# Squares and products of a two-layer transformer kernel placed on VectorE or GpSimd by the kernel's planner

## The chip, the cores and the metric

The kernel runs on one core of a Trainium2 chip. The time is that of one execution on the device in microseconds (us); the kernel before took 835.92 us, the median of three runs (835.25 to 836.88). The engines are called as in the profile: PE is TensorE (matmuls), PEld its weight loads, DVE is VectorE, ACT is ScalarE, POOL is GpSimd, SP is the engine whose queue issues the DMAs.

## The reference

Two layers, each of attention and a squared-ReLU network, over x of [1, 2048, 448] in bf16, with 16 heads of 28 columns and 1792 hidden units; both layers share their weights.

```python
def _A_ref(x, wqkv, wo):
    qkv = (x @ wqkv).reshape(B, S, 3, H, Dh).transpose(2, 0, 3, 1, 4)
    q, k, v = qkv[0], qkv[1], qkv[2]
    scores = jnp.einsum("bhqd,bhkd->bhqk", q, k) * Dh ** -0.5
    p = _softmax(scores, axis=-1)
    o = jnp.einsum("bhqk,bhkd->bhqd", p, v)
    return o.transpose(0, 2, 1, 3).reshape(B, S, D) @ wo

def _B_ref(x, w1, b1, w2, b2):
    h = jnp.einsum("bsd,df->bsf", x, w1) + b1
    r = jnp.where(h > 0, h, 0)
    return jnp.einsum("bsf,fd->bsd", r * r, w2) + b2

x = x + _A_ref(_layernorm(x), A_wqkv, A_wo)
x = x + _B_ref(_layernorm(x), B_w1, B_b1, B_w2, B_b2)
# and both lines once more
```

## The kernel before

**Work and tiles.** The 16 heads are four groups of four; a head has 32 rows of the array, so four heads share it. A *bank* is one PSUM bank of scores: 128 partitions by 512 fp32, which is one head with 256 queries and two blocks of 128 keys. PE makes the scores of three banks (`s_stream`, L956) into one of two tiles `sc`. The exponentials of a bank go one of two ways:

- On ACT: one activation (`e_stream`, L986) makes bf16 weights `pt` of all three banks of a tile, or of two banks when the third goes the other way.
- On VectorE's route: `a_unit` and `a_rest` make the exponential by bit arithmetic in four steps. The first step on DVE (L1034) shifts and clamps the scores into an fp32 tile in SBUF (`v_w`, or a piece of `K_sb`) and with that frees the PSUM bank. POOL (L1051) makes a linear function of the low 16 bits, in bf16 (`pd`, which lies in `pt`, `V_sb`, `h` or a tile of its own). DVE squares that in place (L1057, `bend`). DVE's closing step (L1064) adds the two and writes the bits of the bf16 result.

Then PE multiplies the weights with V (`p_stream`, L1127); 32 columns of V hold 28 of the head and ones, which give the sums of the softmax. For most blocks of 256 queries the result is copied to SBUF (L1154, L1156), the sums go through small DMAs on SP's queue and come back as inverse sums spread over partitions, and one product (`norm_pair`, L1255) for each pair of groups writes `oTn`. `chain` takes it from there: matmuls with wo, the addition to x (L1264), layer norm (L528, L533 on DVE; L555, L556 on POOL for the inverse root; L649 on DVE), W1 with ReLU (L1322) and square (L1331) on DVE, W2, again L1264, and for layer 1 the layer norm and the Q, K and V of layer 2. The work of `chain` runs beside the attention of later blocks, so that ACT has exponentials from start to end.

**What sets the order.** The program is written by a planner in Python (`Planner.run`). Each step is an `Op` with an engine, an estimated duration, what it depends on and what buffer it takes; streams of Ops have priorities. The planner always emits the Op that can start earliest by its own clocks. The engines then run their lists in this order. What matters here:

- `port=True` marks Ops of DVE and POOL that it does not let start while the other engine runs an Op so marked; it then moves the start to the end of that Op. L1051, L1057, L1064, L1255, L1331 and L649 are so marked.
- An Op may have several engines; `earliest` then takes the first, unless a later one could start earlier by more than a margin.
- `apart` decides whether a bank goes VectorE's route. One of its conditions is that DVE's queue in the plan is below an entry of the table `PACE`, which has 128 entries over the length of the program:

```python
if max(0.0, pl.clock["DVE"] - now) + left[0] > PACE[i * len(PACE) // len(units)]:
    return None
```

- `warm` adds up PE's load over the last 1.8 us (`TICK`); where it is low, `heat` (L1552) and `s_stream` emit matmuls whose result is not used, to keep PE's clock up. An Op's load is 0.9 (`SHARE`) of its duration unless its field `w` says otherwise.
- `sums` (L406) makes column sums of W1 once, between the layers, by 56 matmuls of one column; the last half block needs them.

Of the kernel before, what the change touches and what calls it, by code (L numbers as in the profile page):

```python
# [13 lines left out]
ALU = mybir.AluOpType  # L14
# [17 lines left out]
SHARE = 0.9  # L32
YL = 0.05
GN = 0.718
GM = 1.275
GS = 1.3
NORMG = 0
GM_ON = 0
GS_ON = 0
GS_STOP = 100  # L40
EXP_MID = 0.50773
EXP_LOW = 128.0 * 128
EXP_SHIFT = 184.0 * 128
# [39 lines left out]
LEAD = 15  # L83
LAST = 690
BUSY = 0.995
PACE = (2.2, 2.2, 2.2, 2.2, 1.8, 2.2, 2.2, 1.4, 3.0, 1.4, 1.4, 1.4, 2.2, 3.2, 3.6, 2.2, 2.2, 2.2, 2.2, 2.2, 0.6, 3.4, 2.6, 1.8, 1.0, 1.8, 2.6, 2.6, 2.2, 3.8, 3.0, 2.2, 2.2, 3.6, 2.2, 0.6, 3.0, 1.8, 1.8, 1.8, 1.8, 2.6, 2.2, 2.2, 1.4, 3.4, 2.6, 1.0, 2.2, 3.4, 3.6, 3.6, 1.4, 2.2, 3.0, 2.6, 3.8, 3.4, 1.8, 1.0, 2.6, 2.6, 2.2, 2.2, 3.8, 3.0, 1.8, 1.0, 3.8, 3.0, 1.8, 2.2, 2.2, 1.4, 3.2, 4.4, 2.6, 3.6, 3.6, 1.4, 1.8, 3.6, 3.0, 3.0, 3.0, 3.0, 2.2, 2.2, 2.2, 2.2, 3.0, 3.0, 1.8, 2.2, 2.6, 2.6, 1.4, 1.4, 4.0, 3.6, 3.6, 1.8, 1.8, 2.2, 2.2, 3.6, 1.4, 1.4, 2.2, 4.0, 1.8, 1.4, 2.2, 1.8, 2.6, 2.6, 2.2, 2.2, 2.6, 2.2, 2.8, 3.2, 1.4, 1.8, 1.8, 2.2, 2.2, 2.2)
SPAN = 11
NPT = 11
NOS = 2
# [39 lines left out]


class Op:
    __slots__ = ("eng", "dur", "fn", "deps", "acq", "rel", "mode", "sets", "start", "end", "res", "turn", "ready", "lat", "need", "got", "more", "room", "port", "base", "w")

    def __init__(self, eng, dur, fn, deps=(), acq=None, rel=None, mode="full", sets=(), lat=0.0, need=1, port=False):
        self.eng = eng if isinstance(eng, tuple) else (eng,)
        self.dur, self.fn, self.deps, self.mode, self.lat = dur, fn, deps, mode, lat
        self.rel = rel if isinstance(rel, list) else ([] if rel is None else [rel])
        self.acq = acq if isinstance(acq, tuple) or callable(acq) else (() if acq is None else (acq,))
        self.sets = sets if isinstance(sets, list) else ([sets] if sets else [])
        self.start = self.end = self.res = self.turn = None  # L140
        self.need, self.got, self.more, self.port, self.base = need, [], 0.0, port, None
        self.w = None
# [5 lines left out]
class Planner:  # L148
# [28 lines left out]
    def earliest(self, o):  # L177
        t = o.base
        if t is None:
            t = 0.0  # L180
            for d in o.deps:
                if not isinstance(d, Op):
                    d = self.tok.get(d)
                if d is None or d.end is None:
                    return None, None
                same = d.eng[0] == o.eng[0] and len(o.eng) == 1
                t = max(t, d.end + d.lat + ((0.03 if same else 0.10) if d.eng[0] == "DVE" else
                                    (0.0 if same and d.eng[0] != "DMA" else LAT[d.eng[0]])))
            o.base = t
        acq = o.acq() if callable(o.acq) else o.acq  # L190
        if o.acq:
            free = [r.when() for r in acq if r.when() is not None]
            if not free:
                return None, None
            t = max(t, min(free))
        o.ready = t
        best = None
        for e in o.eng:
            s = max(t, self.clock[e])
            if e == "PE" and self.mode != o.mode:  # L200
                s = max(t, self.clock[e] + 0.1)
            if o.port and e in self.ports:
                for a, b in self.ports["POOL" if e == "DVE" else "DVE"]:
                    if a <= s < b:
                        s = b
            if best is None or s < best[0] - 0.05:
                best = (s, e)
        return best

    def run(self):  # L210
        while self.streams:
            cands = []
            for st in self.streams:
                s, e = self.earliest(st[2]) if st[2] is not None else (None, None)
                if s is not None:
                    cands.append((s, st[0](s) if callable(st[0]) else st[0], e, st))
            assert cands, "no stream can go on"
            known = cands

            due = next((c[3][2].ready for c in cands if c[1] == 0), None)  # L220
            if due is None:
                due = next((c[0] + c[3][2].dur + LAT["ACT"] for c in cands if c[1] == 1), None)
            if due is not None:
                ok = [c for c in cands if c[2] != "PE" or c[1] == 0 or c[0] + c[3][2].dur <= due + self.slack()]
                cands = ok or cands
            s, _, e, st = min(cands, key=lambda c: (max(c[3][2].ready, self.clock[c[2]]) if c[2] == "PE" and self.turns() else c[0], c[1]))
            o = st[2]
            o.eng = (e,)
            if o.acq:
                o.res = min((r for r in (o.acq() if callable(o.acq) else o.acq) if r.when() is not None), key=lambda r: r.when())  # L230
                o.turn = len(o.res.rel)
                o.res.rel.append(None)
            o.start, o.end = s, s + o.dur
            if e == "PE":
                o.room = min([c[0] for c in known if c[2] == "PE" and c[3] is not st] or [1e9]) - o.end
            if o.fn:
                o.fn(e)
            o.end += o.more
            self.clock[e] = o.end - (OVER if e == "DVE" and o.dur > 0.1 else 0.0)
            if e == "PE":  # L240
                self.mode = o.mode
            if o.port and e in self.ports:
                self.ports[e] = [*self.ports[e][-5:], (s, o.end)]
            if e == "PE" and o.end > s:
                self.used = [u for u in self.used if u[1] > s - 2 * TICK] + [(s, o.end, SHARE * o.dur if o.w is None else o.w)]
            if e in self.past:
                self.past[e] = [p for p in self.past[e] if p[1] > s - 40.0] + [(s, max(s, self.clock[e]))]
            for a in o.rel:
                a.got.append(o.end + o.lat + LAT[e])
                if len(a.got) == a.need:  # L250
                    a.res.rel[a.turn] = max(a.got)
            for key in o.sets:
                self.tok[key] = o
            st[2] = next(st[1], None)
            if st[2] is None:
                self.streams.remove(st)
# [3 lines left out]
def kernel(  # L260
# [12 lines left out]
    nc = tc.nc  # L273
# [56 lines left out]
    more = [const.tile([P, QR], DT.float32, name=f"more{g}") for a in AHEAD[3:] for g in a]  # L330
# [63 lines left out]
    def sums():  # L394
# [5 lines left out]
        def add(e, fcs):  # L400
            if fcs[0] == 0:
                box["t"] = bank(first, "mt")
            for fc in fcs:
                for dc in range(NDC):
                    k = DL if dc == NDC - 1 else P
                    nc.tensor.matmul(box["t"][:, fc:fc + 1], lhsT=w1[0:k, dc, fc * P:(fc + 1) * P], rhs=onec[0:k, :],  # L406
                                     start=fc == 0 and dc == 0, stop=fc == NFC - 1 and dc == NDC - 1)
        first = last = None
        for f in range(0, NFC, 2):
            fcs = range(f, f + 2)  # L410
            last = Op("PE", 0.48, lambda e, fcs=fcs: add(e, fcs), deps=[("w1",)] if first is None else [last], acq=spare(8) if first is None else None)
            first = first or last
            yield last

# [405 lines left out]
    units = []  # L820
    for pi, (l, qb, g, kbs, first, last) in enumerate(passes):
        r = 4 // blocks[l][qb][1]
# [8 lines left out]
    at = [0]  # L831
# [212 lines left out]
    def a_rest(gi, c, box, unit):  # L1044
# [9 lines left out]

        def bend(e):
            pd = gbuf[gi]["pd"]
            nc.vector.tensor_tensor(out=pd, in0=pd, in1=pd, op=ALU.mult)  # L1057
        h = Op("DVE", 0.42, bend, deps=[y], port=True)
        yield h
        left[0] -= 0.34  # L1060

# [12 lines left out]
    oTn_of = {}  # L1074
# [144 lines left out]
    def norm_pair(l, qb, g, pair):  # L1219
# [34 lines left out]
        def mul(e):  # L1254
            (nc.gpsimd if e == "POOL" else nc.vector).tensor_tensor(out=oTn_of[l, qb][0][:, g:g + 2, 0:n], in0=both,  # L1255
                                    in1=box["r"][:, :, 0:n], op=ALU.mult)
        m = Op("POOL" if GM_ON else "DVE", GM if GM_ON else 0.13 + 2 * n / 930, mul, deps=[r, oTn_of[l, qb][1]], rel=pair["own"], port=True)
        yield m
        yield Op("DVE", 0.0, None, deps=[m], rel=r)
        norm_end(l, qb, m, 2)  # L1260
# [6 lines left out]
    def chain(l, qb):  # L1267
# [43 lines left out]
        for f0 in range(0, NFC, pack):  # L1311
# [20 lines left out]

            def then(o, b=b, square=square):
                aside = not s_left and (l, qb) == (1, len(blocks[1]) - 2)
                pool = GS_ON and f0 // pack % GS_ON == 1 and len(units) - at[0] > GS_STOP
                b["s"] = Op("ACT" if aside else "POOL" if pool else "DVE", 0.5 if aside else GS if pool else 0.42, square, deps=[o], rel=o, port=True)
                return [b["s"]]
            o = yield from mm_tile(
                [(i * n, n, [(w1[:, dc, fc * P:(fc + 1) * P], xnT[:, dc, 0:n], *([ends[dc // 2]] if split else [])) for dc in range(NDC)])
# [264 lines left out]
```

## Time and profile before

| | |
|---|---|
| median of three runs | 835.92 us (835.25 to 836.88) |
| the profiled execution | 836.43 us |
| its span in the profile | 834.4 us |
| ACT busy | 815.2 us, 98% |
| DVE busy | 793.5 us, 95% |
| PE busy | 780.0 us, 93% |
| POOL busy | 234.8 us, 28% |
| mean granted clock of PE | 0.992 |

The span runs from the first to the last instruction of the program; the time of the execution is longer by what lies around it. A group of instructions in the profile has a line, an engine, what it writes and reads, and its shape; then the busy time, the mean length of one in ns, and the idle time of the engine just before them with what ended it. Instructions of one engine can overlap, so that count times mean can be more than the busy time. Names such as `V_sb` or `K_sb` appear for steps of VectorE's route because these tiles' spare parts serve as its buffers.

### The profile page before, as it was taken

To read this page: it belongs to the slowest core of one execution; us is meant where nothing else is said; L and a number is where in the kernel's file an instruction comes from. 1 tells how busy PE (TensorE), PEld (TensorE's weight loads), DVE (VectorE), ACT (ScalarE), POOL (GpSimd) and SP (SyncE) were. 2 spreads that over 40 slices of the span, in tenths; PEclk is the share of its full clock that TensorE was granted. 3 is DMA by queue.
4 is the path that set the end of the run, shared out by engine and by line. 5 is a ranking of instruction groups with operands and counts; after the bars stand their busy time and mean duration, and the time that the engine had idled before them with its cause. 6 is when DMAs were issued, how large, how long until landed. Compare 5 with 4: busy or idle time off the path is not lost.

```text
span 834.4 us, 26688 instructions
## 1 busy us (share of the span) xinstructions
PE 780.0 (93%) x11403; PEld 405.6 (49%) x11403; DVE 793.5 (95%) x1646; ACT 815.2 (98%) x700; POOL 234.8 (28%) x366
## 2 busy tenths in 40 slices
PE   8999889999999999998999999989999999999997
PEld 4445545554444455444444544435454544545565
DVE  7999999999999999999999999999999999999955
ACT  8999999999999999999999999999999999999993
POOL 3222232233223232322223223332223132242200
PEclk9999999999999999999999999699999999999999
DMA  9200100000000000000000000011000000000000
GB/s 247 75 2 3 28 16 15 15 15 16 15 3 14 15 15 16 15 5 12 2 2 2 2 2 3 16 29 29 24 18 20 20 26 21 21 16 12 21 14 13
DMA packets 32359, 17.88 MB, mean 21 GB/s; under 512 B 17833, under 2 KB 31787, under 8 KB 32240
## 3 DMA queue, kind: packets, MB, share of 16 engines
q1 hardware_dynamic: 32240, 16.18, 7.0%
q8 instruction: 89, 1.46, 0.7%
q14 instruction: 30, 0.25, 0.1%
HBM read 13.88 MB, written 2.07 MB: 19 GB/s over the span
## 4 chain that ended last, share of the span: by engine, by line
DVE 40%; ACT 26%; PE 25%; issue 8%; DMA 0%; POOL 0%; ACTq 0%; DVEq 0%
ACT pt L986 26%; PE mt L686 10%; PE sc L956 8%; DVE v_w L1034 6%; DVE pt L1064 5%; PE oT L1127 4%; DVE r L1322 4%; DVE pt L1057 3%; DVE K_sb L1034 3%; DVE V_sb L1064 2%; DVE x_sb L1264 2%; DVE V_sb L1331 1%; DVE h L1064 1%; DVE V_sb L1057 1%; DVE xn L649 1%
## 5 line engine op out<-in xcount | busy, mean ns | idle before, releaser
L986 ACT ACTIVATE pt<-sc 128x1536 bf16<-128x1536 f32 (+1 forms) x683 | 803.8, 1407 | 4.3 <-PE sc L956 3.3
L956 PE MATMUL sc<-Q_sb,K_sb 32*128 32x256 bf16 (+1 forms) x4412 | 278.4, 267 | 36.0 <-ACT pt L986 28.6
L956 PEld LDWEIGHTS <-K_sb 32*128 32x128 bf16 x4412 | 106.6, 92 | 213.3 <-issue 154.7
L1127 PE MATMUL oT<-pt,V_sb 128*32 128x256 bf16 (+1 forms) x4004 | 154.8, 270 | 1.1 <-DVE K_sb L596 0.4
L1034 DVE TENSOR_SCALAR v_w<-sc 128x512 f32<-128x512 f32 x194 | 131.2, 681 | 4.1 <-PE sc L956 3.3
L686 PE MATMUL mt<-xnT,w 128*128 128x256 bf16 (+1 forms) x872 | 116.4, 272 | 3.6 <-DVE r L1322 0.9
L1127 PEld LDWEIGHTS <-V_sb 128*32 128x32 bf16 x4352 | 91.8, 96 | 53.8 <-issue 47.9
L1051 POOL TENSOR_SCALAR pt<-v_w 128x512 bf16<-128x512 uint16 x85 | 61.4, 723 | 158.6 <-DVE v_w L1034 138.5
L686 PEld LDWEIGHTS <-w 128*128 128x128 bf16 x896 | 75.8, 98 | 37.2 <-issue 28.2
L1322 DVE TENSOR_SCALAR r<-mt 128x512 bf16<-128x512 f32 x107 | 72.5, 680 | 2.6 <-PE mt L686 2.3
L1051 POOL TENSOR_SCALAR V_sb<-v_w 128x512 bf16<-128x512 uint16 x54 | 39.2, 726 | 101.6 <-DVE v_w L1034 101.4
L686 PE MATMUL mt<-w,V_sb 128*128 128x448 bf16 x260 | 66.9, 355 | 0.0
L1064 DVE SCALAR_TENSOR_TENSOR pt<-v_w,pt 128x512 int16<-128x512 f32 x85 | 57.2, 680 | 0.0
L1034 DVE TENSOR_SCALAR K_sb<-sc 128x512 f32<-128x512 f32 x78 | 52.9, 680 | 2.4 <-PE sc L956 1.9
L1057 DVE TENSOR_TENSOR pt<-pt 128x512 bf16<-128x512 bf16 x109 | 49.1, 463 | 0.0
L1264 DVE TENSOR_TENSOR x_sb<-x_sb,mt 128x448 bf16<-128x448 bf16 x61 | 37.1, 609 | 5.5 <-PE mt L686 5.3
L1057 DVE TENSOR_TENSOR V_sb<-V_sb 128x512 bf16<-128x512 bf16 x89 | 40.1, 460 | 0.0
L528 DVE BATCH_NORM_STATS2 st<-x_sb 128x6 f32<-128x448 bf16 x63 | 38.6, 614 | 1.6 <-DMA x_sb<-in_A_x_dram 1.2
L1051 POOL TENSOR_SCALAR V_sb<-K_sb 128x512 bf16<-128x512 uint16 x35 | 24.6, 703 | 51.7 <-DVE K_sb L1034 44.3
L1064 DVE SCALAR_TENSOR_TENSOR V_sb<-v_w,V_sb 128x512 int16<-128x512 f32 x54 | 37.5, 694 | 0.1
L686 PEld LDWEIGHTS <-V_sb 128*128 128x128 bf16 x302 | 24.5, 98 | 25.7 <-issue 12.6
L1051 POOL TENSOR_SCALAR h<-v_w 128x512 bf16<-128x512 uint16 x29 | 20.5, 708 | 45.1 <-DVE v_w L1034 44.3
(141 smaller groups left out, 911.1 us busy)
## 6 DMA issues: line engine op xcount, KB each, us to landing
rec<-scr SPq DMA_DIRECT2D x54, 128.0 KB
x_sb<-in_A_x_dram SPq DMA_DIRECT2D x8, 224.0 KB
out_dram<-x_sb SPq DMA_DIRECT2D x15, 112.0 KB
w<-in_B_w_dram SPq DMA_DIRECT2D x1, 1568.0 KB
w<-in_B_w_dram SPq DMA_DIRECT2D x1, 1344.0 KB
dn<-oT_sb SPq DMA_DIRECT2D x54, 4.0 KB
V_sb<-in_A_wqkv_dram SPq DMA_DIRECT2D x4, 168.0 KB
scr<-dn SPq DMA_DIRECT2D x27, 8.0 KB
```

The costliest lines, as they stand in the source:

```text
L528: nc.vector.bn_stats(out=box["st"][:, :], in_=x_sb[:, t0 + j, :] if src is None else src())
L649: nc.vector.tensor_scalar(out=xn[:, 0:D], in0=x_sb[:, t0 + j, :], scalar1=mv[0][:, j, 0:1], scalar2=ln[j], op0=ALU.subtract, op1=ALU.mult)
L686: nc.tensor.matmul(box["t"][:, c0:c0 + n], lhsT=lhsT() if callable(lhsT) else lhsT, rhs=rhs, start=a, stop=b)
L956: nc.tensor.matmul(dst[k][:, i * nt * P:(i + 1) * nt * P], lhsT=K_sb[l][rows, g, (kb + i) * P:(kb + i + 1) * P], rhs=Q_sb[rows, g, t0 * P: ...
L986: t = nc.scalar.activation(out=pt[:, 0:n], in_=gbuf[gi]["sc"][:, 0:n], func=AF.Exp, scale=float(np.log(2.0)) * 2.0 ** -FRAC)
L1034: t = nc.vector.tensor_scalar(out=box["w"], in0=two(src), scalar1=EXP_SHIFT, scalar2=EXP_LOW, op0=ALU.add, op1=ALU.max)
L1051: nc.gpsimd.tensor_scalar(out=two(pd), in0=low, scalar1=-EXP_MID * 65536, scalar2=EXP_BEND, op0=ALU.add, op1=ALU.mult)
L1057: nc.vector.tensor_tensor(out=pd, in0=pd, in1=pd, op=ALU.mult)
L1064: nc.vector.scalar_tensor_tensor(out=two(pd.bitcast(DT.int16)), in0=box["w"], scalar=EXP_BITS, in1=two(pd), op0=ALU.add, op1=ALU.add)
L1127: nc.tensor.matmul(box["t"][DHP * hh:DHP * hh + DHP, 0:n], lhsT=V_sb[l][:, kb + i, 4 * g + hh, :], rhs=p[:, c0:c0 + n], start=begin and kb ...
L1264: nc.vector.tensor_tensor(out=x_sb[:, tb, lo:hi], in0=x_sb[:, tb, lo:hi], in1=t[:, 0:hi - lo], op=ALU.add)
L1322: nc.vector.tensor_scalar(out=r[:, 0:w], in0=t[:, 0:w], scalar1=0.0, scalar2=None, op0=ALU.max)
```

## The change

`bend`, the square of VectorE's route, may now be on DVE (0.416 us in the plan) or on POOL (1.28, `GB`), and so may the product with the inverse sums in `norm_pair` (on POOL 0.2 + 2n/477 us in the plan). The planner takes POOL where it could start more than 0.8 us (`AWAY`) earlier than DVE. For the square of the ReLU the same choice is written in, but switched off (`S_ANY = 0`). The earlier switches for fixed shares on POOL, which were off, are gone. The matmuls of the column sums of W1 have a load of 0.02 instead of 0.9 of their duration. The table `PACE` has 128 new entries (mean 2.36, before 2.38). As the planner decides by its clocks, the order of all engines' lists changes too. The lines of the changed kernel stand three or four further down than those of the kernel before.

```diff
-GM = 1.275
-GS = 1.3
+AWAY = 0.8
+B_ANY = 1
+M_ANY = 1
+S_ANY = 0
+GB = 1.28
...
-GM_ON = 0
-GS_ON = 0
-GS_STOP = 100
...
@@ class Op
-        self.dur, self.fn, self.deps, self.mode, self.lat = dur, fn, deps, mode, lat
+        self.durs = dur if isinstance(dur, dict) else None
+        self.dur, self.fn, self.deps, self.mode, self.lat = max(dur.values()) if self.durs else dur, fn, deps, mode, lat
@@ Planner.earliest
-            if best is None or s < best[0] - 0.05:
+            if best is None or s < best[0] - (AWAY if o.durs else 0.05):
                 best = (s, e)
@@ Planner.run
+            if o.durs:
+                o.dur = o.durs[e]
             o.start, o.end = s, s + o.dur
@@ sums
             last = Op("PE", 0.48, lambda e, fcs=fcs: add(e, fcs), deps=[("w1",)] if first is None else [last], acq=spare(8) if first is None else None)
+            last.w = 0.02
@@ a_rest
         def bend(e):
             pd = gbuf[gi]["pd"]
-            nc.vector.tensor_tensor(out=pd, in0=pd, in1=pd, op=ALU.mult)
-        h = Op("DVE", 0.42, bend, deps=[y], port=True)
+            (nc.gpsimd if e == "POOL" else nc.vector).tensor_tensor(out=pd, in0=pd, in1=pd, op=ALU.mult)
+        h = Op(("DVE", "POOL"), {"DVE": 0.416, "POOL": GB}, bend, deps=[y], port=True) if B_ANY else Op("DVE", 0.416, bend, deps=[y], port=True)
@@ norm_pair
-        m = Op("POOL" if GM_ON else "DVE", GM if GM_ON else 0.13 + 2 * n / 930, mul, deps=[r, oTn_of[l, qb][1]], rel=pair["own"], port=True)
+        m = Op(("DVE", "POOL") if M_ANY else "DVE", {"DVE": 0.13 + 2 * n / 930, "POOL": 0.2 + 2 * n / 477} if M_ANY else 0.13 + 2 * n / 930, mul, deps=[r, oTn_of[l, qb][1]], rel=pair["own"], port=True)
@@ chain
-                pool = GS_ON and f0 // pack % GS_ON == 1 and len(units) - at[0] > GS_STOP
-                b["s"] = Op("ACT" if aside else "POOL" if pool else "DVE", 0.5 if aside else GS if pool else 0.42, square, deps=[o], rel=o, port=True)
+                b["s"] = Op("ACT" if aside else ("DVE", "POOL") if S_ANY else "DVE", 0.5 if aside else {"DVE": 0.416, "POOL": GB} if S_ANY else 0.416, square, deps=[o], rel=o, port=True)
```

More of the change, by code (lines that the diff above doesn't have):

```diff
@@ L85 @@
 BUSY = 0.995
-PACE = (2.2, 2.2, 2.2, 2.2, 1.8, 2.2, 2.2, 1.4, 3.0, 1.4, 1.4, 1.4, 2.2, 3.2, 3.6, 2.2, 2.2, 2.2, 2.2, 2.2, 0.6, 3.4, 2.6, 1.8, 1.0, 1.8, 2.6, 2.6, 2.2, 3.8, 3.0, 2.2, 2.2, 3.6, 2.2, 0.6, 3.0, 1.8, 1.8, 1.8, 1.8, 2.6, 2.2, 2.2, 1.4, 3.4, 2.6, 1.0, 2.2, 3.4, 3.6, 3.6, 1.4, 2.2, 3.0, 2.6, 3.8, 3.4, 1.8, 1.0, 2.6, 2.6, 2.2, 2.2, 3.8, 3.0, 1.8, 1.0, 3.8, 3.0, 1.8, 2.2, 2.2, 1.4, 3.2, 4.4, 2.6, 3.6, 3.6, 1.4, 1.8, 3.6, 3.0, 3.0, 3.0, 3.0, 2.2, 2.2, 2.2, 2.2, 3.0, 3.0, 1.8, 2.2, 2.6, 2.6, 1.4, 1.4, 4.0, 3.6, 3.6, 1.8, 1.8, 2.2, 2.2, 3.6, 1.4, 1.4, 2.2, 4.0, 1.8, 1.4, 2.2, 1.8, 2.6, 2.6, 2.2, 2.2, 2.6, 2.2, 2.8, 3.2, 1.4, 1.8, 1.8, 2.2, 2.2, 2.2)
+PACE = (2.2, 2.2, 2.2, 1.4, 1.4, 1.0, 1.4, 1.4, 3.0, 1.4, 2.2, 2.2, 2.2, 3.0, 2.6, 1.4, 1.8, 1.8, 3.0, 3.0, 3.0, 1.8, 1.4, 2.6, 2.6, 1.8, 2.2, 2.2, 3.8, 3.4, 3.2, 2.8, 0.6, 1.4, 2.6, 1.4, 2.6, 2.6, 2.2, 2.6, 2.2, 2.2, 1.4, 1.4, 3.6, 4.0, 1.4, 1.4, 2.6, 2.6, 1.0, 1.8, 3.0, 3.0, 2.2, 2.2, 2.2, 2.2, 1.4, 1.4, 2.6, 2.6, 1.8, 1.8, 3.8, 1.4, 1.4, 3.6, 3.6, 3.6, 2.8, 3.0, 3.0, 2.6, 3.2, 4.4, 1.8, 0.6, 1.8, 1.8, 1.8, 2.6, 2.6, 2.6, 3.0, 3.4, 1.4, 1.4, 1.4, 3.0, 3.0, 1.8, 1.8, 2.2, 2.6, 1.8, 1.4, 1.0, 2.2, 3.6, 2.8, 2.6, 2.6, 1.0, 2.6, 2.6, 2.6, 3.0, 2.6, 4.0, 3.6, 2.6, 2.6, 3.0, 3.0, 2.2, 2.6, 1.8, 1.0, 2.6, 4.4, 3.6, 4.4, 2.6, 2.6, 1.8, 2.2, 2.2)
 SPAN = 11
@@ L131 @@
 class Op:
-    __slots__ = ("eng", "dur", "fn", "deps", "acq", "rel", "mode", "sets", "start", "end", "res", "turn", "ready", "lat", "need", "got", "more", "room", "port", "base", "w")
+    __slots__ = ("eng", "dur", "fn", "deps", "acq", "rel", "mode", "sets", "start", "end", "res", "turn", "ready", "lat", "need", "got", "more", "room", "port", "base", "w", "durs")
     def __init__(self, eng, dur, fn, deps=(), acq=None, rel=None, mode="full", sets=(), lat=0.0, need=1, port=False):
         self.eng = eng if isinstance(eng, tuple) else (eng,)
-        self.dur, self.fn, self.deps, self.mode, self.lat = dur, fn, deps, mode, lat
+        self.durs = dur if isinstance(dur, dict) else None
+        self.dur, self.fn, self.deps, self.mode, self.lat = max(dur.values()) if self.durs else dur, fn, deps, mode, lat
         self.rel = rel if isinstance(rel, list) else ([] if rel is None else [rel])
```

## The prediction

> **What bounds the kernel now.** I read the page's parts first: busy shares, the row of granted clock, the chain, the costliest groups.
>
> ```profile
> PE 780.0 (93%) x11403; PEld 405.6 (49%) x11403; DVE 793.5 (95%) x1646; ACT 815.2 (98%) x700; POOL 234.8 (28%) x366
> PEclk9999999999999999999999999699999999999999
> DVE 40%; ACT 26%; PE 25%; issue 8%; DMA 0%; POOL 0%; ACTq 0%; DVEq 0%
> L986 ACT ACTIVATE pt<-sc 128x1536 bf16<-128x1536 f32 (+1 forms) x683 | 803.8, 1407 | 4.3 <-PE sc L956 3.3
> L956 PE MATMUL sc<-Q_sb,K_sb 32*128 32x256 bf16 (+1 forms) x4412 | 278.4, 267 | 36.0 <-ACT pt L986 28.6
> L1034 DVE TENSOR_SCALAR v_w<-sc 128x512 f32<-128x512 f32 x194 | 131.2, 681 | 4.1 <-PE sc L956 3.3
> L1051 POOL TENSOR_SCALAR pt<-v_w 128x512 bf16<-128x512 uint16 x85 | 61.4, 723 | 158.6 <-DVE v_w L1034 138.5
> ```
>
> ACT's exponentials take 803.8 us with 4.3 us of idle time among them; PE waits 28.6 us for ACT's banks. So ACT sets the pace, with VectorE (DVE) close behind: the chain changes between DVE, ACT and PE, and DVE is hardly ever idle. GpSimd (POOL) is idle for 72%, mostly waiting for DVE's first step (L1034). A bank of scores that ACT need not do shortens the stage, if DVE can bear it.
>
> The stages, as busy time of each engine in stretches (columns: length, PE, PEld, DVE, ACT, POOL, granted clock, DMA share, GB/s):
>
> ```profile
> 0.00:10.00 10.00, 7.77 (x41) 4.34 (x42) 6.34 (x28) 7.96 (x11) 4.77 (x13) 1.00 0.77 204
> 700.00:800.00 100.00, 94.85 (x1657) 51.90 (x1660) 97.97 (x205) 99.35 (x85) 27.92 (x37) 1.00 0.06 19
> 800.00:834.40 34.40, 29.49 (x604) 19.96 (x592) 16.29 (x50) 21.51 (x20) 1.31 (x3) 1.00 0.05 16
> ...
> 529.50:543.20 13.70, 13.70 (x165) 5.34 (x168) 11.64 (x25) 11.81 (x11) 4.76 (x7) 0.51 0.09 23
> ```
>
> In the middle DVE and ACT are both within 2% of full. The last row is the one dip of PE's clock, at the column sums of W1 (525 to 534 us): 13.7 us at half the clock, in which ACT stands idle for 13.70 - 11.81 = 1.9 us.
>
> **Part 1, ACT: fewer banks.** In the instruction lists of the two programs the exponentials over three banks go from 410 to 391 and those over two from 273 to 292: 19 banks leave ACT, and the banks that VectorE's route takes go from 272 to 291. By shape:
>
> ```profile
> L986 ACT ACTIVATE pt<-sc 128x1536 bf16<-128x1536 f32 x410 | 592.5, 1577 | 2.8 <-PE sc L956 2.2 <-PE oT L1127 0.2
> L986 ACT ACTIVATE pt<-sc 128x1024 bf16<-128x1024 f32 x273 | 291.7, 1152 | 1.5 <-PE sc L956 1.2
> ```
>
> A bank is 1577 - 1152 = 425 ns, so ACT loses 19 x 0.425 = **8.1 us**. It lies on the path, as ACT is idle for only 4.3 us among its exponentials.
>
> **Part 2, DVE: squares go, banks come.** Of the squares (L1057) 116 stay on DVE and 175 are on POOL; of 28 products with inverse sums (L1255) 3 are on POOL. DVE's prices:
>
> ```profile
> 399.65 0.75 DVE L1057 TENSOR_TENSOR pt<-pt 128x512 bf16<-128x512 bf16 x2
> 400.32 1.28 DVE L1064 SCALAR_TENSOR_TENSOR pt<-v_w,pt 128x512 int16<-128x512 f32 x2
> L1057 DVE TENSOR_TENSOR pt<-pt x109: 354/414/834, 121.3 to 765.5; 128x512 bf16<-128x512 bf16 x109
> L1255 DVE TENSOR_TENSOR oTn<-oT_sb,rec x28: 413/681/1067, 101.9 to 795.0; 128x512 bf16<-128x512 f32 x27, 128x256 bf16<-128x256 f32 x1
> ```
>
> Instructions in a row overlap: two squares fill 0.75 us where one has a median of 0.414, so a square costs DVE 0.34; two closing steps (L1064) fill 1.28, so one costs about 0.60, and the first step and the product, of the same 0.68, as much. DVE loses 272 - 116 = 156 squares (53.0 us) and 3 products (1.8); it gains 19 first steps and 19 closing steps (22.8). One relu and one square at the end move to ACT (1.0), behind the exponentials. Net: **33 us less work on DVE**, before waits.
>
> **Part 3, POOL: the price of a square there.** No trace row shows one.
>
> ```profile
> L1051 POOL TENSOR_SCALAR pt<-v_w x85: 619/620/1584, 117.9 to 759.5; 128x512 bf16<-128x512 uint16 x85
> L555 POOL TENSOR_TENSOR ve<-mv,eps_t x33: 191/198/551, 4.4 to 800.1; 128x2 f32<-128x2 f32 x30, 128x1 f32<-128x1 f32 x3
> ```
>
> From below: POOL's one-source instruction of the same size, 0.62 us. From above: 1.58, the longest that this instruction ever took, waits included. Between them: the floor of a two-element instruction is 0.2, the 512 elements of one source add 0.42, two sources twice that: 1.04. I take 1.28, the planner's own cost in the diff (GB), which is nearer to 1.04 than to either end. POOL then has 291 x 0.62 + 175 x 1.28 + 3 x 1.27 = 408 us of such work and about 39 us of small things (now 234.8 less 272 x 0.72): 447 us, 54% of the span; 60% at 1.58. POOL itself does not become the bound.
>
> The Trainium skill (GPSIMD Engine Reference, section 3.1) gives about 2.6 cycles at 1.2 GHz for an element of a two-source instruction; 512 of them over the 0.2 floor would be 1.31, an estimate, which would change the sum by 5 us of POOL's idle time.
>
> **Part 4, what the two engines do to each other.** This is the real cost.
>
> ```profile
> 391.81 0.66 POOL L1051 TENSOR_SCALAR pt<-v_w 128x512 bf16<-128x512 uint16 x1 [0.28 <-DVE v_w L1034]
> 391.91 0.83 DVE L1057 TENSOR_TENSOR V_sb<-V_sb 128x512 bf16<-128x512 bf16 x1
> 44.30 0.68 DVE L1064 SCALAR_TENSOR_TENSOR V_sb<-v_w,V_sb 128x512 int16<-128x512 f32 x1
> 44.47 0.99 POOL L1051 TENSOR_SCALAR V_sb<-v_w 128x512 bf16<-128x512 uint16 x1 [1.20 <-DVE v_w L1034]
> ```
>
> A square that starts on DVE while POOL has 0.56 us to run takes 0.83 in place of 0.41: it waits 0.42. POOL's instruction waits likewise behind DVE's closing step (0.99 in place of 0.62). The first step, which reads PSUM, keeps its 0.68. So DVE's instructions with SBUF sources alone (squares, closing steps, L1331, L649, L1255) and POOL's exclude each other.
>
> The Trainium skill (SBUF — State Buffer, section "SBUF: two separate sides") has the loser fully blocked for the whole instruction. The trace agrees on who waits, not on how long: 0.42 of the remaining 0.56. By the page's rule each such meeting would cost 0.14 more.
>
> What it costs DVE now, from group means against medians:
>
> ```profile
> L1057 DVE TENSOR_TENSOR pt<-pt 128x512 bf16<-128x512 bf16 x109 | 49.1, 463 | 0.0
> L1057 DVE TENSOR_TENSOR V_sb<-V_sb 128x512 bf16<-128x512 bf16 x89 | 40.1, 460 | 0.0
> L1064 DVE SCALAR_TENSOR_TENSOR h<-v_w,h 128x512 int16<-128x512 f32 x29 | 21.3, 736 | 0.0
> L649 DVE TENSOR_SCALAR xn<-x_sb,mv,rstd 128x448 bf16<-128x448 bf16 x63 | 27.6, 461 | 1.2 <-POOL rstd L556 0.7 <-PE mt L1552 0.5
> ```
>
> The squares lose about 48 ns each, 13 us in all; closing steps, norms and the rest I put at about as much: 25 us. The exposure grows: POOL's instructions of this kind fill 169 us now (272 x 0.62), 408 then, and the mean time that one still has to run when DVE comes rises from 0.31 to 0.49 us; DVE's instructions that can be caught fall from 742 (272 squares, 272 closing steps, 107 L1331, 63 L649, 28 L1255) to 601. In proportion (number x share of some 808 us x rest): 742 x 0.21 x 0.31 = 48 against 601 x 0.50 x 0.49 = 147, so 25 us become 76: **51 us more waiting at worst**. At best nothing is added. I take 30, for two reasons in the code: the planner does not start one of these instructions in the other engine's time and gives DVE another one, and it hands DVE a bank only while DVE's queue in the plan is under the entry of PACE, so that 291 is what a plan with full exclusion could still bear, where the chip's is milder by 0.14 a time.
>
> DVE then needs 793.5 - 33 + 30 = 790.5 us. Of its 40.9 us of idle time 3.7 lie before 10 us and 18.1 after 800; with 5 more for the rest, a DVE that sets the pace ends at 790.5 + 27 = 817.5, before ACT. So ACT stays the bound, with more small gaps: the 4.3 us, less the 1.9 of the dip, are 2.4 now; I add **1.5**.
>
> The new wait is that of the closing step for a square on POOL, about 0.9 us longer than on DVE. Behind it on DVE queue first steps and evacuations; the first step frees a bank that PE's next scores need, and ACT needs those. On POOL the next L1051 and the two instructions of a layer norm's inverse root queue behind a square. SP's queue keeps its 190 entries.
>
> **Part 5, column sums.** They weigh 0.02 instead of 0.9 x 0.48 in the planner's measure of PE's load; heating matmuls (L1552) rise from 99 to 106, 7 x 0.19 = 1.3 us, hidden in PE's waits for ACT. If the dip goes, ACT regains its 1.9 us. But the list still has runs of sums and scores with no heating until the last sums, so I take half: **-1.0**, ends 0 and -1.9.
>
> **Part 6, the end.** After the last exponential PE's list has 16 more matmuls of W1 and 4 more of W2, and 13 fewer of 32 columns.
>
> ```profile
> 824.63 1.95 PE L1488 MATMUL mt<-xnT,w 128*128 128x128 bf16 x32
> 822.12 1.86 PE L686 MATMUL sc<-w,V_sb 128*128 128x448 bf16 x9
> ```
>
> 16 x 0.06 + 4 x 0.19, less 0.2, is 1.5 us; PE is idle for 34.4 - 29.5 = 4.9 us after 800 us and can hide some: **+1.0**, ends 0 and 1.5.
>
> **The sum.** The profiled execution took 836.4 (span 834.4 and 2.0 around it): 836.4 - 8.1 - 1.0 + 1.0 + 1.5 = 829.8. It lies 0.5 above the median of 835.9, so the forecast for the median is **829.3**.
>
> **Rivals.**
> A, slower: the exclusion makes DVE the bound. For it speaks that DVE already runs at 98% in the middle; against it, the 33 us of relief and the planner's care. With S us of added waiting DVE ends at 793.5 - 33 + 27 + S = 787.5 + S. It passes ACT's path (827.8) at S = 40 and the span of before at S = 47. The proportional 51 gives a span of 838.5, 840.0 as a median; POOL's dearer 1.58 would push it well past 845. The Trainium skill (Perfetto Trace Analysis, "Optimizing Scalar/DVE Operations") says that moving work between these two engines might not help, as they share a port; by that this rival holds.
> B, no change: the exclusion delays first steps just enough that ACT idles for what it gained, S near 45: 835.
> C, faster still: no new gaps, the dip gone, the end hidden: 836.4 - 8.1 - 1.9 - 0.5 = 825.9.
>
> **How the numbers follow.** Forecast 0.56, C 0.12, B 0.09, A 0.23. A measurement of this kernel can tell 0.2%, 1.7 us, from no change: faster means under 834.2, slower over 837.6. Forecast and C are faster, 0.68; B the same, 0.09; A slower, 0.23. The range goes from C, 826, to just past A's 840: 841, leaving out a little of C and the dearer half of A. The faster cases alone lie in 826 to 833.
>
> **What would show it.** Right: L986 at about 795.7 us with idle time of 3 to 6 us; L1057 on POOL near 1.28; DVE near 790 us; clock row without a 6 or with a milder one. Wrong: idle time before L986 over 10 us with L956 as releaser and DVE's L1034 behind that, mean L1064 over 800 ns, DVE over 800 us; or squares on POOL well over 1.4 us.

## The result: 880.55 us, 5.4% slower

The changed kernel takes 880.55 us (median; 879.24 to 884.09) against 835.59 of the kernel before in the same comparison: a ratio of 1.0544, 95% interval 1.0508 to 1.0579. The forecast was 829.3, the range 826 to 841. The direction was rival A's, the size beyond its 840. The page of the changed kernel, in the prediction's order (busy shares, granted clock, chain, groups):

```profile
span 879.3 us, 26911 instructions
PE 791.4 (90%) x11410; PEld 402.0 (46%) x11410; DVE 836.1 (95%) x1523; ACT 820.4 (93%) x702; POOL 461.3 (52%) x563
PEclk9999999999989999999999999899999999999999
DVE 61%; PE 21%; issue 8%; ACT 8%; DMA 1%; POOL 1%; SPq 0%; DVEq 0%; ACTq 0%; POOLq 0%
L990 ACT ACTIVATE pt<-sc 128x1536 bf16<-128x1536 f32 (+1 forms) x683 | 808.0, 1297 | 45.1 <-PE sc L960 38.7
L1068 DVE SCALAR_TENSOR_TENSOR pt<-v_w,pt 128x512 int16<-128x512 f32 x82 | 66.9, 822 | 0.0
L1061 POOL TENSOR_TENSOR pt<-pt 128x512 bf16<-128x512 bf16 x74 | 86.3, 1170 | 4.4
L1335 DVE TENSOR_TENSOR V_sb<-r 128x512 bf16<-128x512 bf16 x66 | 40.2, 616 | 0.3
```

DVE runs 123 instructions fewer than before and is busy for 42.6 us more (836.1 against 793.5). Its share of the chain goes from 40% to 61%, and ACT now stands idle for 45.1 us ahead of its exponentials, waiting for PE's scores. PE's scores wait for DVE in turn (groups of waits of the changed kernel: engine, line, waited for, us in total, times, longest):

```profile
PEld L960 <- DVE v_w L1038: 47.7, 95, 1.5
ACT pt L990 <- PE sc L960: 38.7, 78, 2.2
PE sc L960 <- DVE v_w L1038: 15.1, 30, 1.3
```

L1038 is DVE's first step, which frees the PSUM bank for the next scores. It comes late because instructions ahead of it in DVE's list take longer: in the groups shown, the closing step (L1068) 822 ns on the mean, where 680 was the mean in the kernel before, the square of the ReLU (L1335) 616 instead of 440. The same two groups before:

```profile
L1064 DVE SCALAR_TENSOR_TENSOR pt<-v_w,pt 128x512 int16<-128x512 f32 x85 | 57.2, 680 | 0.0
L1331 DVE TENSOR_TENSOR V_sb<-r 128x512 bf16<-128x512 bf16 x67 | 29.2, 440 | 0.5
```

The long middle stretch of the kernel before (length, PE, PEld, DVE, ACT, POOL, granted clock, DMA share, GB/s):

```profile
10.00:800.00 790.00, 742.76 (x10777) 381.27 (x10778) 770.92 (x1571) 785.70 (x671) 228.73 (x350) 0.99 0.07 19
```

The same stretch of the changed kernel, and what follows it:

```profile
10.00:800.00 790.00, 715.23 (x9941) 353.25 (x9939) 770.74 (x1370) 750.76 (x637) 431.45 (x520) 0.98 0.07 19
800.00:879.30 79.30, 68.85 (x1434) 44.51 (x1428) 59.13 (x128) 61.55 (x55) 25.10 (x31) 0.97 0.05 13
```

From 10 to 800 us DVE is busy for 770.9 us before and 770.7 after, the same 97.6%, with 1370 instructions in place of 1571. What it did not get done is made up for after 800 us. The span grew by 44.9 us: 42.6 of DVE's busy time and 2.3 of its idle time.

Where DVE's busy time comes from is seen in single instructions (the timeline of the changed kernel: start, length, engine and line, and in brackets the idle time before with what ended it):

```profile
45.57 1.04 POOL L1061 TENSOR_TENSOR V_sb<-V_sb 128x512 bf16<-128x512 bf16 x1
45.90 1.26 DVE L1068 SCALAR_TENSOR_TENSOR V_sb<-v_w,V_sb 128x512 int16<-128x512 f32 x1
...
59.45 1.04 POOL L1061 TENSOR_TENSOR V_sb<-V_sb 128x512 bf16<-128x512 bf16 x1
59.62 1.43 DVE L1068 SCALAR_TENSOR_TENSOR V_sb<-v_w,V_sb 128x512 int16<-128x512 f32 x1
```

A closing step that meets a square on POOL with 0.71 us left to run takes 1.26, one that meets 0.87 us takes 1.43, in place of 0.68: it waits for the rest of the square, less 0.12 to 0.13 us. This is the rule: of the changed kernel's closing steps 60 start with 0.2 to 1.0 us of a square still to run, and each of them took 0.678 us and the rest of the square, less 0.13. I call **waiting** what DVE's closing steps, squares of banks, squares of the ReLU, layer norms and products took in all above the median of an unhindered one (0.678, 0.411, 0.412, 0.387, 0.678 us). Before it is 28.8 us, after **104.2**: 45.1 in closing steps, 20.5 and 21.1 in the two kinds of squares, 10.7 in norms, 6.8 in products. With the prediction's 33 us of less work, 793.5 - 33 + 75.4 = 835.9; measured 836.1. That it fits to 0.2 us is luck: the same sum for the first experiment below, 793.5 - 33 + 3.2, is 6.6 us under what was measured there.

### The profile page after: what moved, and what is told of

It reads as the page before. It is cut to its first block, busy times and chain, and to the rows that moved or that the text cites. A ratio compares the mean times of both kernels' runs of the same rounds, so it can differ in the third digit from the quotient of the medians.

```text
span 879.3 us, 26911 instructions
## 1 busy us (share of the span) xinstructions
PE 791.4 (90%) x11410; PEld 402.0 (46%) x11410; DVE 836.1 (95%) x1523; ACT 820.4 (93%) x702; POOL 461.3 (52%) x563
## 4 chain that ended last, share of the span: by engine, by line
DVE 61%; PE 21%; issue 8%; ACT 8%; DMA 1%; POOL 1%; SPq 0%; DVEq 0%; ACTq 0%; POOLq 0%
PE mt L690 9%; DVE v_w L1038 9%; ACT pt L990 7%; DVE pt L1068 7%; PE sc L960 6%; DVE r L1326 5%; DVE V_sb L1068 5%; PE oT L1131 4%; DVE K_sb L1038 4%; DVE V_sb L1335 3%; DVE x_sb L1268 3%; DVE xn L653 3%; DVE pd L1068 2%; DVE st L532 2%; DVE pt L1061 2%
## 5 line engine op out<-in xcount | busy, mean ns | idle before, releaser
L990 ACT ACTIVATE pt<-sc 128x1536 bf16<-128x1536 f32 (+1 forms) x683 | 808.0, 1297 | 45.1 <-PE sc L960 38.7
L960 PE MATMUL sc<-Q_sb,K_sb 32*128 32x256 bf16 (+1 forms) x4412 | 280.6, 269 | 36.1 <-DVE v_w L1038 15.1
L960 PEld LDWEIGHTS <-K_sb 32*128 32x128 bf16 x4412 | 98.5, 92 | 224.0 <-issue 137.6
L1038 DVE TENSOR_SCALAR v_w<-sc 128x512 f32<-128x512 f32 x209 | 140.5, 676 | 3.8 <-PE sc L960 3.4
L1055 POOL TENSOR_SCALAR pt<-v_w 128x512 bf16<-128x512 uint16 x82 | 57.1, 697 | 98.3 <-DVE v_w L1038 71.7
L1055 POOL TENSOR_SCALAR V_sb<-v_w 128x512 bf16<-128x512 uint16 x76 | 55.8, 735 | 74.4 <-DVE v_w L1038 70.7
L1061 POOL TENSOR_TENSOR pt<-pt 128x512 bf16<-128x512 bf16 x74 | 86.3, 1170 | 4.4
L1061 POOL TENSOR_TENSOR V_sb<-V_sb 128x512 bf16<-128x512 bf16 x62 | 73.9, 1193 | 3.9
L1326 DVE TENSOR_SCALAR r<-mt 128x512 bf16<-128x512 f32 (+1 forms) x107 | 72.1, 674 | 2.9 <-PE mt L690 2.7
L690 PE MATMUL mt<-w,V_sb 128*128 128x448 bf16 (+2 forms) x288 | 68.9, 346 | 0.0
L1068 DVE SCALAR_TENSOR_TENSOR pt<-v_w,pt 128x512 int16<-128x512 f32 x82 | 66.9, 822 | 0.0
L1068 DVE SCALAR_TENSOR_TENSOR V_sb<-v_w,V_sb 128x512 int16<-128x512 f32 x76 | 61.5, 812 | 0.1
L1038 DVE TENSOR_SCALAR K_sb<-sc 128x512 f32<-128x512 f32 x82 | 55.2, 678 | 3.6 <-PE sc L960 3.4
L1055 POOL TENSOR_SCALAR pt<-K_sb 128x512 bf16<-128x512 uint16 x37 | 25.8, 698 | 36.7 <-DVE K_sb L1038 27.1
L1335 DVE TENSOR_TENSOR V_sb<-r 128x512 bf16<-128x512 bf16 x66 | 40.2, 616 | 0.3
L1055 POOL TENSOR_SCALAR h<-v_w 128x512 bf16<-128x512 uint16 x25 | 20.3, 811 | 33.7 <-DVE v_w L1038 33.1
```

What stands on the lines that cost most here:

```text
L690: nc.tensor.matmul(box["t"][:, c0:c0 + n], lhsT=lhsT() if callable(lhsT) else lhsT, rhs=rhs, start=a, stop=b)
L960: nc.tensor.matmul(dst[k][:, i * nt * P:(i + 1) * nt * P], lhsT=K_sb[l][rows, g, (kb + i) * P:(kb + i + 1) * P], rhs=Q_sb[rows, g, t0 * P: ...
L990: t = nc.scalar.activation(out=pt[:, 0:n], in_=gbuf[gi]["sc"][:, 0:n], func=AF.Exp, scale=float(np.log(2.0)) * 2.0 ** -FRAC)
L1038: t = nc.vector.tensor_scalar(out=box["w"], in0=two(src), scalar1=EXP_SHIFT, scalar2=EXP_LOW, op0=ALU.add, op1=ALU.max)
L1055: nc.gpsimd.tensor_scalar(out=two(pd), in0=low, scalar1=-EXP_MID * 65536, scalar2=EXP_BEND, op0=ALU.add, op1=ALU.mult)
L1068: nc.vector.scalar_tensor_tensor(out=two(pd.bitcast(DT.int16)), in0=box["w"], scalar=EXP_BITS, in1=two(pd), op0=ALU.add, op1=ALU.add)
```

## The experiments

Theory 1, from these rows: the exclusion between POOL's squares and DVE costs the whole loss. Rivals: ACT and PE got worse by the new order or the new table, or POOL's length holds up the closing steps.

**The exclusion taken away, the plan kept.** Each square on POOL becomes five instructions of four columns, so that POOL is as long busy but never in one long instruction; the other 492 columns stay unsquared.

```diff
-            (nc.gpsimd if e == "POOL" else nc.vector).tensor_tensor(out=pd, in0=pd, in1=pd, op=ALU.mult)
+            if e == "POOL":
+                for c in range(0, 20, 4):
+                    nc.gpsimd.tensor_tensor(out=pd[:, c:c + 4], in0=pd[:, c:c + 4], in1=pd[:, c:c + 4], op=ALU.mult)
+                return
+            nc.vector.tensor_tensor(out=pd, in0=pd, in1=pd, op=ALU.mult)
```

> The changed kernel with the same order and the same 175 squares on GpSimd, but each of these multiplies only 20 of its 512 columns, as five instructions of four columns (about 0.2 us each, so about 1.0 us of GpSimd as before); the other 492 columns are left unsquared. Theory 1 (exclusion: a square on GpSimd shuts out VectorE's instructions with SBUF sources for its whole length): the waiting goes, VectorE's closing step falls from a mean of 820 to 690-720 ns, VectorE busy from 836 to 760-780 us, ACT idle before exponentials from 45 to under 15 us, time 828 to 840. Theory 2 (lateness: the square takes longer on GpSimd, so that the closing step comes late and holds up the queue): GpSimd's queue is as long as before, so 865 or more. Theory 3 (the new table or the new weight made a bad order): nothing changes, 870 or more.

Measured: 829.08 us, 0.9917 of before (0.9886 to 0.9948). From its page and its groups:

```profile
PE 778.7 (94%) x11410; PEld 404.5 (49%) x11410; DVE 770.3 (93%) x1523; ACT 808.8 (98%) x702; POOL 450.2 (54%) x1263
L990 ACT ACTIVATE pt<-sc 128x1536 bf16<-128x1536 f32 (+1 forms) x683 | 796.3, 1388 | 4.5 <-PE sc L960 3.1
L1063 POOL TENSOR_TENSOR pt<-pt 128x4 bf16<-128x4 bf16 x370 | 85.4, 268 | 4.3
```

POOL is about as busy as after (450.2 against 461.3 us), the five instructions of a square together take about as long as the one (85.4 us busy for the 74 squares of this group, 86.3 in the changed kernel; single ones overlap), the plan is the changed kernel's, and the loss is gone: waiting 32.0 us, DVE 770.3, ACT's idle time 4.5. So neither the new order nor POOL's length costs the 51 us between the two kernels; the exclusion does.

**The same plan with every square on DVE.** If POOL's squares were worth having in spite of the waiting, taking them back would cost.

```diff
-            (nc.gpsimd if e == "POOL" else nc.vector).tensor_tensor(out=pd, in0=pd, in1=pd, op=ALU.mult)
+            nc.vector.tensor_tensor(out=pd, in0=pd, in1=pd, op=ALU.mult)
```

> The changed kernel's plan and order, with every square emitted on VectorE (291 of them), the planner still believing that 175 are on GpSimd. Theory 1: VectorE gets 175 x 0.34 = 60 us of work and loses some 70 us of waiting, so it stays the bound: VectorE busy 820-840, time 855 to 880, about as the changed kernel. Theory 2: the squares are quick again, so most of the 45 us come back: under 850. Theory 3: 870 to 890.

Measured: 864.6 us, 1.0339 (1.0312 to 1.0366), 16 us less than the changed kernel; waiting 37.7. From its page:

```profile
PE 787.2 (91%) x11410; PEld 402.9 (47%) x11410; DVE 825.0 (96%) x1698; ACT 818.9 (95%) x702; POOL 267.1 (31%) x388
```

DVE has 175 squares more and is 11.1 us less busy than after. In this plan a square on POOL costs DVE more than a square of its own: (104.2 - 37.7) / 175 = 0.38 us waited, and 0.34 us saved by the prediction's price, or (66.5 - 11.1) / 175 = 0.32 by these two runs.

**Why the planner did not see it.** `earliest` moves a start out of the other engine's marked Ops, but tests the start alone. An Op that begins before a marked Op already placed and runs into it passes. That happens here because `AWAY` lets a square stay DVE's candidate for up to 0.8 us, in which DVE gets other steps; then it is put on POOL, beginning ahead of them. In the plan of before, marked Ops of the two engines (POOL's step for the inverse root of a layer norm, L555 and L556, is marked too) lie over each other 8 times, 3.3 us in all; in the plan of after 162 times, 90 us. The test of the whole Op:

```diff
-                for a, b in self.ports["POOL" if e == "DVE" else "DVE"]:
-                    if a <= s < b:
+                for a, b in sorted(self.ports["POOL" if e == "DVE" else "DVE"]):
+                    if a <= s < b or o.durs and s <= a < s + o.durs[e]:
```

> The changed kernel with one line of the planner changed: a step with two engines may not cover the start of a step of the other engine that is already placed. The plan then has 74 squares on GpSimd, 276 banks on VectorE's route and hardly any overlap of the two engines. Theory 1: VectorE's waiting is 25 to 45 us and the time 832 to 845. Theory 2: 74 of 175 late squares, so 45 x 74/175 = 19 us over the kernel before: about 855. Theory 3: 870 or more.

Measured: 864.22 us, 1.0337 (1.031 to 1.0364). Only 74 squares are left on POOL, and waiting falls to 63.2 us, while the span is still 25.2 us above the end of its plan (836.3). Theory 1 alone gave 832 to 845, so a second cause exists. Instruction by instruction (the n-th in the plan and the n-th in the trace), 44 of the 74 squares started ahead of the DVE instruction that the plan has before them, and held DVE up for some 20 to 25 us, by how much of a meeting is counted. Nothing in the program binds the two: their data have nothing to do with each other, and each engine starts when its own list and data allow.

**That cause alone.** GpSimd reads two elements of what that DVE instruction wrote, so the square can't start earlier. `DLOG` lists DVE's squares and closing steps as they are written into the program; norms and products are not in it.

```diff
+    def keep_order(op):
+        before = [x for x in DLOG[-8:] if op.start - 2.0 < x[0].end <= op.start + 0.02]
+        if before:
+            a = max(before, key=lambda x: x[0].end)[1]
+            nc.gpsimd.tensor_tensor(out=seen_t[:, :], in0=a, in1=a, op=ALU.mult)
...
+            if e == "POOL":
+                keep_order(h)
...
```

> The plan with the whole check (74 squares on GpSimd), and before each of these squares GpSimd reads two elements of what VectorE's instruction wrote that the plan put just ahead of it, so that it cannot overtake that instruction. Theory R (race: the plan's order between the two engines is enforced by nothing, a square that is ready early overtakes a late VectorE instruction and shuts it out for 1 us): the 44 such meetings go, VectorE's waiting falls from 63 to about 40 us and the time from 864 to 845-855. Theory N (no room: the squares have to wait somewhere, the wait only moves to GpSimd and comes back as late closing steps): 860 or more.

Measured: 847.72 us, 1.0134 (1.011 to 1.0158), waiting 40.9. The page's first part and a group of squares on POOL, with the whole check alone:

```profile
PE 789.4 (92%) x11474; PEld 405.9 (47%) x11474; DVE 806.3 (94%) x1575; ACT 822.2 (95%) x705; POOL 341.2 (40%) x448
L1061 POOL TENSOR_TENSOR pt<-pt 128x512 bf16<-128x512 bf16 x33 | 39.2, 1190 | 1.9
```

The same two rows with the order kept as well:

```profile
PE 787.0 (93%) x11474; PEld 407.4 (48%) x11474; DVE 785.9 (93%) x1575; ACT 817.4 (97%) x705; POOL 341.1 (40%) x514
L1075 POOL TENSOR_TENSOR pt<-pt 128x512 bf16<-128x512 bf16 x33 | 34.7, 1050 | 0.2
```

With the same plan DVE loses 20.4 us of busy time, and POOL's squares no longer wait either: 1190 ns become 1050. One square of the 74 still overtakes. So the race between the engines is shown: the plan is the same, and only the order of these squares is bound.

**The order kept for POOL's linear function of the low 16 bits as well** (`keep_order` also ahead of this step, L1055 of the changed kernel, which overtakes DVE too, some 80 times in the kernel above).

```diff
+            keep_order(y)
             low = box["w"].bitcast(DT.uint16)
```

> The same with GpSimd's first instruction of each bank (276 of them) held back likewise. Theory R: nearly all unplanned meetings go, VectorE's waiting is 25-40 us; GpSimd has some 350 tiny instructions of 0.2 us more, which its idle time covers; 838 to 852. Theory N: VectorE's waiting falls but ACT's and PE's idle time does not; 860 or more.

Measured: 851.45 us, 1.0179 (1.0152 to 1.0206); waiting 37.7, ACT's idle time 15.5 against 12.0. L1055 is the start of the chain that ends in the closing step; holding it saves 3 us of waiting, and the time is 3.7 us longer. Where that is lost was not separated.

**The price of a square in the plan put right** (whole check, and the measured length).

```diff
-GB = 1.28
+GB = 1.05
```

> The plan with the whole check and the square on GpSimd priced at the 1.05 us that it was measured at, in place of 1.28. Theory R: GpSimd no longer runs ahead of the plan behind each square, fewer overtakings: VectorE's waiting 45 to 55 us, 850 to 860. Theory N: no change, 860 to 868.

Measured: 861.34 us, 1.0301 (1.0277 to 1.0324), waiting 61.6. The price was not the trouble: the planner placed 69 squares on POOL, not more, and 46 of them overtook.

**The rest of the change alone**: the table and the weight with nothing on POOL, and then the weight alone, with the table `PACE` of before as well.

```diff
-B_ANY = 1
-M_ANY = 1
+B_ANY = 0
+M_ANY = 0
```

> The changed kernel with all squares and products on VectorE (both switches 0): only the new table and the new weight of the column sums are left. Theories 1 and 2: 834 to 846, a table made for another plan costs a few us. Theory 3: 865 or more.

> The edit: the kernel before with nothing but the new weight of the column sums of W1 (0.02), its old table of banks, and no square or product on GpSimd. The prediction's part 5: PE's clock does not fall at the column sums, and about 1 us is gained, at most 1.9: 834.0 to 835.6. Rival: the dip stays, as in the runs so far, and the weight, which sets when scores are started, makes the old table a poor one for the new plan (which ends at 839.3 us against 830.7): a median of 842 to 848, with VectorE's waiting at 28 to 30 us as before.

Measured: 848.88 us, 1.0148 (1.0114 to 1.0183), and 846.0 us, 1.0117 (1.0103 to 1.0131). Both have little waiting (28.5 and 30.7 us) and take some 13 and 10 us more than the kernel before; the first is beyond the 834 to 846 expected. The weight does not keep PE's clock up (stretches of the kernel with the weight alone):

```profile
531.00:533.00 2.00, 2.00 (x22) 1.36 (x22) 2.00 (x5) 1.71 (x2) 0.99 (x1) 0.50 0.00 0
533.00:535.00 2.00, 2.00 (x34) 1.01 (x32) 1.49 (x3) 1.75 (x2) 0.00 (x0) 0.50 0.03 8
535.00:537.00 2.00, 2.00 (x24) 0.92 (x20) 1.25 (x3) 1.09 (x2) 0.05 (x1) 0.50 0.02 1
```

It halves between 531 and 537 us with ACT idle for 0.29 + 0.25 + 0.91 = 1.45 us; in the changed kernel it is half from about 547 to 557. The dip is shorter than before in these two (6.9 and 10.2 us, 13.6 before), but it lasts 17.1 us in the kernel that keeps the order of both steps, with the same weight. And the weight changes when scores start: with the old table the plan itself ends 8.6 us later (839.3 against 830.7), so that a table made for another plan no longer fits.

**A table searched for the planner with the whole check**, with the order kept (`keep_order` ahead of the squares) and without. Beside the whole check the edit is another set of 128 entries in `PACE`, found by changing a few at a time and keeping what brought the plan's end forward. The weight of the column sums and `GB` are those of the changed kernel.

> The edit: the planner with the check of the whole instruction, a table of banks (PACE) searched anew for that planner (the plan ends at 826.0 us, against 830.7 in the plan of before and 836.3 in the one of whole_check; 87 squares on GpSimd), and the read of two elements ahead of each square on GpSimd that keeps it behind the VectorE instruction that the plan has before it. Theory 1 with the race (an order between the two engines that nothing enforces costs the rest): the span should stand to the plan's end as in the kernel with the kept order and the old table, 843.9 against 836.3, so 833.6, a median of 832 to 838, VectorE's waiting 35 to 45 us. Rival: squares on GpSimd are worth having once their order is kept and the table fits, and the time falls clearly below that of before: under 832. Other rival: 87 reads and squares make the first steps' copies of bits on GpSimd late, over 842.

> The edit: as the kernel with the searched table and the kept order, but without the reads that keep the order, so that a square on GpSimd may overtake the VectorE instruction that the plan has ahead of it. Theory 1 with the race: the span should exceed the plan's end of 826.0 by about as much as in the first kernel with the whole check, 861.5 against 836.3, so 851, a median of 845 to 858, VectorE's waiting 55 to 70 us, and the difference to the kernel with the kept order 10 to 20 us. Rival (the table decides, and the order matters little): within 4 us of the kernel with the kept order.

Measured: 838.32 us, 1.0029 (1.0019 to 1.0038), and 850.9 us, 1.0179 (1.0163 to 1.0194). The first is just past the upper end of what was expected, and the closest to the kernel before of those that compute everything; the race costs 12.6 us. Nine of the kernels side by side, with the end that the planner itself had for each:

| kernel | squares on POOL | plan's end | span | over the plan | waiting |
|---|---|---|---|---|---|
| before | 0 | 830.7 | 834.4 | 3.7 | 28.8 |
| weight alone | 0 | 839.3 | 843.8 | 4.5 | 30.7 |
| table and weight | 0 | 840.2 | 843.4 | 3.2 | 28.5 |
| whole check, order kept | 74 | 836.3 | 843.9 | 7.6 | 40.9 |
| whole check, order of both steps kept | 74 | 836.3 | 850.0 | 13.7 | 37.7 |
| searched table, order kept | 87 | 826.0 | 835.2 | 9.2 | 36.8 |
| searched table | 87 | 826.0 | 849.0 | 23.0 | 58.4 |
| whole check | 74 | 836.3 | 861.5 | 25.2 | 63.2 |
| after | 175 | 822.3 | 879.3 | 57.0 | 104.2 |

The spans are those of the profiled executions; by the median of each kernel's runs, table and weight is 6.8 us over its plan, the two with the order of the squares kept 9.6 and 10.2, and no other row moves by more than about 1. So the plan is right to 3 to 7 us with no squares on POOL, off by some 10 with the squares' order kept and 13 to 14 with that of both steps, by 23 to 26 without, and by 56 where the squares were also placed over DVE's steps. No version that computes everything beats the kernel before. In the best, 4.7 us of the plan's gain are there on paper, and the other 5.5 us over the plan use them up. POOL's linear function of the low bits still overtakes in it (some 70 times, against some 50 before).

## Why the prediction was wrong

**The step that failed is Part 4's "I take 30".** Measured were 75 us, 45 more, and the span is 44.9 longer than before where about 6.6 less was forecast. The number worked out from rows was 51; it was cut to 30 for a reason in the code, that "the planner does not start one of these instructions in the other engine's time". The sentence is true of starts and says nothing of ends: a square of 1.05 us begins ahead of a closing step and covers it. The other half, "291 is what a plan with full exclusion could still bear", fell too: with the exclusion checked in full, the planner put 276 banks on DVE's route and 74 squares on POOL, and its plan ended 5.6 us after that of before; even the searched table came to 279 banks and 87 squares. And a planned order is not an order on the chip, as the kept order showed.

**Even 51 was no worst case.** The proportional estimate took meetings to fall at random. In the plan of after they don't: of some 100 us by which POOL held DVE up, meeting by meeting, squares on POOL that the plan itself lays over DVE's step account for about 40, squares that overtook for about 26. Most of the rest, some 31, comes from POOL's linear function of the low bits, which made DVE wait 26 before.

**Rival A's mechanism was right**: DVE became the bound, and its signs came as listed (idle time before L990 45.1 us with L960 as releaser and DVE behind that, closing steps at 822 ns, DVE over 800 us). Its formula, 787.5 + S, gives 862.5 for S = 75, 17 us short: it allowed 5 us of idle time for DVE between 10 and 800 us, and DVE keeps 19.3 (790.0 - 770.7), as it did before (19.1). Break-even by the rows was therefore nearer S = 33 than 47.

The Trainium skill (Perfetto Trace Analysis, "Optimizing Scalar/DVE Operations") says that moving work between DVE and GpSimd might not help, as they share a port. The trace agrees and gives the balance: 0.32 to 0.34 us saved and 0.38 waited per square.

**The other terms held**, as the run without exclusion shows. Its exponentials take 796.3 us, 7.5 less (forecast -8.1); idle time among them 4.5 us (forecast 3 to 6); its span is 7.4 less, so the end added about nothing (+1.0 taken, between 0 and 1.5). Its 829.1 us is the forecast's number, for a kernel in which S is 32.0 - 28.8 = 3. The relief of 33 us is the least sure of them: by that run it is 793.5 + 3.2 - 770.3 = 26, by the changed kernel 33. **Part 5** took half of ACT's 1.9 us and got less: the dip of the clock stayed, and ACT is idle in it for 10.3 - 8.8 = 1.5 us in the run without exclusion and 10.2 - 8.9 = 1.3 in the changed kernel.

**POOL's price.** 1.28 was taken; a square that meets nothing is 1.04 (forms and lengths of the changed kernel's squares, min/median/max):

```profile
L1061 POOL TENSOR_TENSOR V_sb<-V_sb x62: 1034/1042/1908, 33.4 to 834.4; 128x512 bf16<-128x512 bf16 x62
L1061 DVE TENSOR_TENSOR V_sb<-V_sb x33: 390/412/1294, 41.0 to 778.1; 128x512 bf16<-128x512 bf16 x33
```

That is the prediction's own worked-out 1.04 from two rows, which should have been taken ahead of the planner's constant. The Trainium skill's rate for two sources (GPSIMD Engine Reference, section 3.1), which gave 1.31 as an estimate, is too dear here: (1042 - 200) / 512 is 1.64 ns an element, 2.0 cycles at that page's 1.2 GHz. POOL's total, forecast at 447 us, is 461.3, waits included.

## What to carry to other kernels

Where two engines exclude each other, cost a move between them as what the giver saves less the other engine's longer hold times the chance of a meeting; if the moved instruction is 2.5 times as long on the other engine, the saving has to be large. A planner's rule is only as good as the test that it makes: read whether it looks at starts or at whole instructions, and what binds the order between two engines in the program, before taking its plan as a bound. A smaller sum of work is no relief where waiting fills it up: DVE was busy for 97.6% of the long stretch before and after. An estimate worked out from rows should not be cut for a reason that no row shows.

## What the runs showed of the hardware

- Of an instruction of DVE with SBUF sources alone and one of POOL, the one that comes second waits for nearly the rest of the other: 1.26 and 1.43 us for a closing step of 0.68 that met 0.71 and 0.87 us, and the rest less 0.13 us in the 60 meetings of a closing step with a square counted above. It holds the other way too: one group of POOL's squares has a mean of 1190 ns with meetings and 1050 with the order kept.
- Short POOL instructions hold DVE up for little: 875 of them, 268 ns on the mean in the group shown, left closing steps at a mean of 730 ns in the run without exclusion, where 175 of 1.05 us had made it 822 and the kernel before has 680 (all of the group pt<-v_w,pt).
- PE's clock halves near the column sums in every kernel here, for 6.8 to 17.1 us (granted clock 0.50), with either load that the planner gave them. What would keep it up was not tried. In the changed kernel it also halves in four other stretches (257.1 to 264.0, 311.7 to 315.2, 612.1 to 615.5 and 830.6 to 834.0 us), which the kernel before and the run without exclusion do not have; what these add to the loss was not separated.
